# Q and K weights loaded as two column halves with x between them, two pads on VectorE, new orders on every engine

## The chip, the cores and the metric

The kernel runs on one core of a Trainium2 chip. The core has five engines that run beside each other, each with its own queue of instructions: TensorE (matmuls; PE in the profile, PEld for its weight loads), VectorE (DVE), ScalarE (ACT), GpSimd (POOL) and SyncE (SP), which here only issues DMA transfers. The metric is the device time of one execution in microseconds. Before the change it is 194.48 us, the median of three runs (193.82 to 194.73).

## The reference

The input x has 2048 rows of 448 columns. The block is a linear-attention layer followed by a gated MLP, each behind a layer norm and with a residual:

```python
phi = lambda t: where(t > 0, t + 1, exp(t)) + 1e-6
q, k, v = split(layernorm(x) @ wqkv)          # 16 heads of 28 columns
kv  = phi(k)^T v          # per head
z   = sum over rows of phi(k)
o   = (phi(q) kv) / (phi(q) z + 1e-6)
h   = x + o @ wo
n   = layernorm(h)
out = h + (gelu(n @ w_gate) * (n @ w_up)) @ w_down     # 1792 inner columns
```

Inputs and the output are bf16.

## The kernel before, in words

The 2048 rows are 16 tiles of 128 rows, numbered 0 to 15. The work has three stretches.

*Attention, first pass (0 to about 34 us).* Each tile of x is loaded (`dx0`, `dx1`, `dx2` for tiles 2 and 3, then `dx4`, `dx8`, `dx12` for four tiles each). Its layer norm is `bnst1_t` and `bnag1_t` on VectorE (lines 409 and 410) and `ln1_t`, `rstd1_t` on ScalarE (416 and 418). The normed rows are made by VectorE for tiles 0 to 3 (`normD_t`, line 431) and transposed by TensorE (`tr0_t` and `tr1_t`, line 439), from where ScalarE and VectorE copy one half each (`evxA_t`, `evxD_t`, lines 444 and 446). For tiles 4 to 15 POOL makes them (`negm1_t`, `normP_t`, lines 413 and 449), and a DMA transpose on SP turns them round (`xT_t`, line 451). The K projection of a tile is `k_t` (four matmuls, line 465), followed by `ek_t` on ScalarE (476) and `ck_t`, `pk_t` on VectorE (477 and 478). The sum over rows that the key-value product needs is gathered by `pt4_t`, or by `pt1_t` and `pt3_t` from tile 10 on (line 484). The Q projection is `q_t`, followed by `eq_t` and `rq_t` on ScalarE (492 and 493), and later by `cq` and `aq` on VectorE.

*The middle (about 34 to 53 us).* `z1`, `z0`, the copies `evp`, `kv` (line 523), `kvm` (527), `w2_0` to `w2_3` (543) with copies `evw` (547 and 549). For the rows: products with z (`t1`, on POOL from row tile 1 on, lines 565 and 581), their sums (`dr`, 568 and 582), the reciprocal (`de`, `rd`) and the scaled rows (`pn`, 572 and 586). For the first pair of tiles TensorE transposes these (`tro`, 595), and `out1` (613) multiplies by w2; later pairs are transposed by DMA (`oT_p`, 601) and multiplied in two halves, `outA_p` and `outB_p` (623 and 624), which need copies of w2 made by two DMAs, `dws0` and `dws1`. `hr_t` (629) adds x; a second norm follows (`bnst2`, `bnag2`, `vpe2`, `pow2`, `negm2`, and `nhD` or `nhP`), `wrap_t` on VectorE (660) doubles the row, and a DMA transpose `hT_t` (661) turns it round. For tiles 0 and 1 TensorE does it (`trh`, 650), with the copies `evhA_0` and `evhD_1`.

*The MLP (53 us to the end).* `gu2_v` and `gu4_v` (lines 722 and 724) are 56 tasks of gate and up matmuls, two half-height matmuls side by side; `ge` on ScalarE (742) and `hm` on VectorE (744) take their results from PSUM, two buffers in turn. `gu2` 0 to 6 serve tiles 0 and 1, 7 to 13 tiles 2 and 3, `gu4` 14 to 27 tiles 4 to 7, 28 to 41 tiles 8 to 11, 42 to 55 tiles 12 to 15. `downA_p` and `downB_p` (692) are the down projection of a pair of tiles, `fo` (698 and 678) adds h, and `do_t` stores the tile. The last two tiles have their own matmuls (674), tile 15 in two column halves.

What sets the order: every operation is a task, numbered in the order in which the code adds it, and `ORDERS` (lines 15 to 49) lists the tasks of each engine in the order in which they are emitted. Nothing is reordered at run time: an instruction that waits holds back everything after it on its engine. The waits come from `_Graph` (lines 69 to 226), which derives them from the buffers that a task reads and writes; a task with several slots (`mw`) waits within itself, so that `q_t` asks for the second half of the transposed tile only at its third matmul and for the last rows of the weights only at its fourth. `HOLD` picks which of several waits is issued first.

Lines that the change touches: the padding memsets and the loads (361 to 373), the helpers `dma_w3` and `dma_w1` (351 to 355: the weights' first 384 rows in three blocks, and the 64 rows left), `proj_reads`, `k_tile`, `q_tile` (468 to 493), `fkv` (519 to 526), `ORDERS` and `HOLD`. Since dwqk_t writes the buffer that the memset wqkpad has written (`b_wqk[1]`), the load waits for the memset.

Of the kernel before, what the change touches and what calls it, by code (L numbers as in the profile page):

```python
# [813 lines left out]
```

## Time and profile before

| what | value |
|---|---|
| three runs | 193.82, 194.48, 194.73 us; median 194.48 |
| profiled execution | 194.29 us, of which the span of its instructions is 192.5 |
| TensorE busy | 185.7 us, 96% of the span; granted clock 1.00 throughout |
| VectorE, ScalarE, POOL busy | 131.5, 77.0, 52.4 us |
| first matmul after the warm-up | 5.39 us |
| x of tiles 2 and 3 landed | 6.91 us |
| k_2 starts | 10.40 us |
| k_7 starts | 21.31 us |
| last K task (pt1_15) over, q_5 starts | 33.61 us |
| first gate/up task (gu2_0) starts | 53.39 us |
| last matmul ends | 190.09 us |

How to read it: the rows of time in the profile are instructions grouped by line; a start and a duration in microseconds from the start of the span, then engine, line, operation, and what was written from what. Where a task is named, it was found by counting the instructions of its engine along `ORDERS`. A matmul's shown duration includes its way through the array, so consecutive matmuls overlap; the step from one start to the next is what TensorE spends: 0.76 us for a `k_t`, `q_t` or `pt4_t`, 1.51 for a `gu` task, 2.65 for a `down` half. The 40 matmuls of the warm-up, 1.04 to 5.49 us, count as busy.

### The profile page before, as it was taken

To read this page: it belongs to the slowest core of one execution; us is meant where nothing else is said; L and a number is where in the kernel's file an instruction comes from. 1 tells how busy PE (TensorE), PEld (TensorE's weight loads), DVE (VectorE), ACT (ScalarE), POOL (GpSimd) and SP (SyncE) were. 2 spreads that over 40 slices of the span, in tenths; PEclk is the share of its full clock that TensorE was granted. 3 is DMA by queue.
4 is the path that set the end of the run, shared out by engine and by line. 5 is a ranking of instruction groups with operands and counts; after the bars stand their busy time and mean duration, and the time that the engine had idled before them with its cause. 6 is when DMAs were issued, how large, how long until landed. Compare 5 with 4: busy or idle time off the path is not lost.

```text
span 192.5 us, 4453 instructions
## 1 busy us (share of the span) xinstructions
PE 185.7 (96%) x1813; PEld 115.3 (60%) x1813; DVE 131.5 (68%) x326; ACT 77.0 (40%) x220; POOL 52.4 (27%) x93
## 2 busy tenths in 40 slices
PE   7999899988999999999999999999999999999995
PEld 7545355544578878975788745556445455555643
DVE  2899997899999986898958774528544624415232
ACT  3798643777992411333214431421442414211200
POOL 8067650740048193340008600001800000000000
PEclk9999999999999999999999999999999999999999
DMA  5974558994388500772200391000095100000045
GB/s 181 382 207 70 100 109 176 220 219 92 84 193 243 95 3 14 86 143 51 48 0 3 60 161 21 2 3 24 0 136 60 51 0 0 3 0 0 3 140 170
DMA packets 34596, 17.11 MB, mean 89 GB/s; under 512 B 26832, under 2 KB 33168, under 8 KB 34576
## 3 DMA queue, kind: packets, MB, share of 16 engines
q1 hardware_dynamic: 34432, 16.72, 39.9%
q8 instruction: 14, 0.23, 0.6%
q10 hardware_dynamic: 144, 0.11, 0.2%
q14 instruction: 6, 0.05, 0.1%
HBM read 8.26 MB, written 1.84 MB: 52 GB/s over the span
## 4 chain that ended last, share of the span: by engine, by line
PE 83%; DVE 8%; DMA 4%; POOL 1%; issue 1%; ACT 1%; SPq 0%; POOLq 0%
PE ps L724 32%; PE ps L692 18%; PE ps L722 13%; PE ps L465 8%; PE ps L484 4%; PE ps L674 3%; PE ps L623 3%; DMA x_sb<-in_A_x_dram 2%; DMA xnT<-xnn 2%; PE ps L624 2%; DVE st L409 1%; DVE den L568 1%; DVE pqn L572 1%; DVE eq L578 1%; PE ps L613 1%
## 5 line engine op out<-in xcount | busy, mean ns | idle before, releaser
L724 PE MATMUL ps<-hnT,wgu_sb 64*128 64x512 bf16 (+1 forms) x490 | 88.7, 333 | 0.0
L722 PE MATMUL ps<-hnT,wgu_sb 64*128 64x512 bf16 (+1 forms) x490 | 88.6, 333 | 0.0
L742 ACT ACTIVATE gl<-ps 128x256 bf16<-128x256 f32 x112 | 36.8, 382 | 83.2 <-PE ps L722 83.2
L744 DVE TENSOR_TENSOR hh<-ps,gl 128x256 bf16<-128x256 f32 x112 | 43.1, 416 | 37.0 <-ACT gl L742 36.8
L724 PEld LDWEIGHTS ps<-hnT,wgu_sb 64*128 64x128 bf16 x490 | 45.1, 94 | 26.2 <-DVE hh L744 2.7
L722 PEld LDWEIGHTS ps<-hnT,wgu_sb 64*128 64x128 bf16 x490 | 45.5, 94 | 5.0 <-DVE hnT L656 0.2
L692 PE MATMUL ps<-wd_sb,hh 64*128 64x448 bf16 x392 | 41.6, 349 | 0.3 <-DVE hh L744 0.3
L692 PEld LDWEIGHTS ps<-wd_sb,hh 64*128 64x128 bf16 x392 | 24.3, 94 | 13.7 <-DVE hh L744 1.3
L465 PE MATMUL ps<-wqk_sb,xnT 128*128 128x448 bf16 x128 | 27.5, 353 | 0.9 <-DMA xnT<-xnn 0.9
L409 DVE BATCH_NORM_STATS2 st<-x_sb 128x6 f32<-128x448 bf16 x32 | 19.1, 614 | 3.8 <-DMA x_sb<-in_A_x_dram 3.7
L465 PEld LDWEIGHTS ps<-wqk_sb,xnT 128*128 128x128 bf16 x128 | 12.1, 98 | 12.3 <-DMA xnT<-xnn 1.3
L581 POOL TENSOR_TENSOR t<-pq,zbc 128x448 f32<-128x448 bf16 x12 | 12.6, 1068 | 16.2 <-DVE pq L579 16.2
L698 DVE TENSOR_TENSOR x_sb<-ps,x_sb 128x448 bf16<-128x448 f32 x14 | 8.4, 618 | 8.9 <-PE ps L692 8.9
L484 PE MATMUL ps<-pk,xnn 128*128 128x448 bf16 x64 | 14.2, 352 | 0.0
L623 PE MATMUL ps<-w,pqnT 64*128 64x448 bf16 x49 | 11.5, 349 | 0.1
L476 ACT ACTIVATE e<-ps 128x448 bf16<-128x448 f32 x16 | 8.7, 541 | 6.7 <-PE ps L465 6.3
L413 POOL TENSOR_SCALAR nm<-mv 128x1 f32<-128x1 f32 (+1 forms) x19 | 4.1, 228 | 25.9 <-DVE mv L410 25.5
L449 POOL TENSOR_SCALAR xnn<-x_sb,nm,rs 128x448 bf16<-128x448 bf16 x12 | 9.6, 797 | 4.6 <-ACT rs L418 4.3
L658 POOL TENSOR_SCALAR hn<-x_sb,nm,rs 128x448 bf16<-128x448 bf16 x14 | 10.4, 751 | 0.5
L624 PE MATMUL ps<-pt_sb,pqnT 64*128 64x448 bf16 x42 | 10.2, 350 | 0.0
L629 DVE TENSOR_TENSOR x_sb<-ps,x_sb 128x448 bf16<-128x448 f32 x16 | 9.7, 614 | 0.7 <-PE ps L624 0.7
L421 POOL TENSOR_SCALAR ln<-mv 128x2 f32<-128x2 f32 x7 | 1.5, 223 | 31.3 <-DVE mv L410 31.1
(83 smaller groups left out, 167.0 us busy)
## 6 DMA issues: line engine op xcount, KB each, us to landing
out_dram<-x_sb SPq DMA_DIRECT2D x15, 112.0 KB, 1.8
wd_sb<-in_B_w_down_dram SPq DMA_DIRECT2D x1, 1568.0 KB, 7.5
x_sb<-in_A_x_dram SPq DMA_DIRECT2D x3, 448.0 KB, 5.6
wgu_sb<-in_B_w_gate_dram SPq DMA_DIRECT2D x1, 896.0 KB, 12.3
wgu_sb<-in_B_w_up_dram SPq DMA_DIRECT2D x1, 896.0 KB, 15.7
wqk_sb<-in_A_wqkv_dram SPq DMA_DIRECT2D x1, 672.0 KB, 4.7
wgu_sb<-in_B_w_gate_dram SPq DMA_DIRECT2D x1, 672.0 KB, 6.2
wgu_sb<-in_B_w_up_dram SPq DMA_DIRECT2D x1, 672.0 KB, 8.7
```

The lines of the kernel that those rows point to most:

```text
L409: op("dve", lambda e: e.bn_stats(st[:, t, :], src_ap), [b_src], [b_st[t]], "bnst%s_%d" % (tag, t))
L465: ins = e.matmul(ps[:, bk, 0:D], xnT[:, t, k, :], wqk_sb[:, k, c0:c0 + D], start=(k == 0), stop=(k == 3))
L484: ins = e.matmul(ps[:, BK_PT[c], 0:D], xnn[:, t % XN_R, c * 128:(c + 1) * 128], pk[:, ip, :], start=(t == 0), stop=(t == T - 1))
L581: op("pool", lambda e, n=n: e.tensor_tensor(t1[:, n, :], pq[:, a + n, :], zbc[:, :], ALU.mult), [b_pq[a + n]] + b_z, [b_t1[n]], "t1p_%d" % ...
L623: e.matmul(ps[:, BK_OUT[0], 0:D], pqnT[ra, i2, sg // 2, :], w2[ra, sg // 2, :], start=(sg == 0), stop=(sg == 5))
L624: ins = e.matmul(ps[:, BK_OUT[1], 0:D], pqnT[rb, i2, 3 + (sg + 1) // 2, :], (w2 if sg == 6 else w2s)[rb, sg // 2, :], start=(sg == 0), sto ...
L658: op("pool", lambda e, t=t, sh=sh: e.tensor_scalar(hn[:, sh, 0:D], x_sb[:, t, :], nm2[:, t:t + 1], rs2[:, t:t + 1], ALU.add, ALU.mult), [b ...
L692: ins = e.matmul(ps[:, BK_O[n], 0:D], hh[rows, j, sl[n]], wd_sb[rows, j, :], start=(half == 0 and j == 0), stop=(half == 1 and j == NJ - 1))
L722: first = e.matmul(psG[:, jj * N:(jj + 1) * N], wgu_sb[A_, k, j * 128:(j + 1) * 128], hnT[A_, ka_, c0:c0 + N], start=(k == 0), stop=(k == ...
L724: ins = e.matmul(psU[:, jj * N:(jj + 1) * N], wgu_sb[B_, k, j * 128:(j + 1) * 128], hnT[B_, kb_, c0:c0 + N], start=(k == 0), stop=(k == NK ...
L742: G.add("act", lambda e, gi=gi, cs_=cs_, psG=psG: e.activation(gl[:, gi, cs_], psG[:, cs_], AF.Gelu_apprx_tanh), r=[b_ps[BK_G[i]]], w=[b_g ...
L744: op("dve", lambda e, dst=dst, srcU=srcU, srcL=srcL: e.tensor_tensor(dst, srcU, srcL, ALU.mult), [b_ps[BK_U[i]], b_glh], [b_ar[j_][t % HR] ...
```

## The change

The code, without the lists of orders:

```diff
-        b_wqk, b_wv = bufs("wqk", 2), bufs("wv", 2)
+        b_wq, b_wk, b_wv = bufs("wq", 2), bufs("wk", 2), bufs("wv", 2)
+        b_wpad = bufs("wpad", 2)
...
         def dma_w3(q, dst, c0, c1, b, name):
-            return dma(q, dst[:, 0:3, :], A_wqkv[0:384, c0:c1].rearrange("(k p) n -> p k n", p=128), [b[0]], name)
+            return dma(q, dst[:, 0:3, c0 % (2 * D):c0 % (2 * D) + c1 - c0], A_wqkv[0:384, c0:c1].rearrange("(k p) n -> p k n", p=128), [b[0]], name)
...
-        for dst, b, nm_ in ((wqk_sb, b_wqk, "wqkpad"), (wv_sb, b_wv, "wvpad")):
-            op("pool", lambda e, dst=dst: e.memset(dst[:, 3, :], 0.0), [], [b[1]], nm_)
+        for dst, b, nm_ in ((wqk_sb, b_wpad[0], "wqkpad"), (wv_sb, b_wpad[1], "wvpad")):
+            op("dve", lambda e, dst=dst: e.memset(dst[B_, 3, :], 0.0), [], [b], nm_)
         dma_x("sp", 0, 1)
-        tx1 = dma_x("act", 1, 2)
-        dma_w3("sp", wqk_sb, 0, 2 * D, b_wqk, "dwqk")
-        dma_w1("sp", wqk_sb, 0, 2 * D, b_wqk, "dwqk_t")
+        dma_x("act", 1, 2)
+        dma_w3("sp", wqk_sb, 0, D, b_wq, "dwq")
+        dma_w1("act", wqk_sb, 0, D, b_wq, "dwq_t")
         dma_x("sp", 2, 4)
+        dma_w3("sp", wqk_sb, D, 2 * D, b_wk, "dwk")
+        tx1 = dma_w1("act", wqk_sb, D, 2 * D, b_wk, "dwk_t")
         dma_x("sp", 4, 8)
...
-        def proj_reads(t):
-            return [(b_xnT[t][0], 0), (b_xnT[t][1], 2), (b_wqk[0], 0), (b_wqk[1], 3)]
+        def proj_reads(t, b):
+            return [(b_xnT[t][0], 0), (b_xnT[t][1], 2), (b[0], 0), (b[1], 3), (b_wpad[0], 3)]
...
-            G.add("pe", lambda e, W: proj(e, W, t, bk, D), r=proj_reads(t), w=[b_ps[bk]], name="k_%d" % t, mw=True)
+            G.add("pe", lambda e, W: proj(e, W, t, bk, D), r=proj_reads(t, b_wk), w=[b_ps[bk]], name="k_%d" % t, mw=True)
...
-        G.add("pe", fkv, r=b_wv + b_pt, w=[b_ps[BK_KV]], name="kv")
+        G.add("pe", fkv, r=b_wv + [b_wpad[1]] + b_pt, w=[b_ps[BK_KV]], name="kv")
```

The Q weights (`dwq`) and the K weights (`dwk`) are separate loads into the same tile, with x of tiles 2 and 3 between them; their last 64 rows (`dwq_t`, `dwk_t`) are issued by ScalarE, ahead of its table load (`tbl1`, line 392). The pads are set by VectorE, on the 64 partitions that the load does not write, and have buffers of their own.

The orders are all new. The stretches that matter, by name:

```
loads on SP
 before  dx0 dwqk dwqk_t dx2 dx4 dx8 dx12 dwv dwv_t dwo
 after   dx0 dwq dx2 dwk dx4 dx8 dx12 dwv dwv_t dwo
start of ScalarE
 before  dx1 tbl1 ln1_0 rstd1_0 ln1_1 rstd1_1 evxA_0 evxA_1 rq_0 eq_0 ln1_2
 after   dx1 dwq_t dwk_t tbl1 ln1_0 rstd1_0 ln1_1 evxA_0 rstd1_1 ln1_2 rstd1_2 eq_0 evxA_1
VectorE, first tiles
 before  bnst1_0 bnag1_0 bnst1_1 bnag1_1 normD_0 normD_1 evxD_0 evxD_1 bnst1_2 bnst1_3 ...
         ck_2 bnst1_9 bnst1_7 bnag1_9 bnag1_7 bnst1_8 pk_2 bnst1_10 ck_3
 after   wqkpad bnst1_0 bnag1_0 bnst1_1 normD_0 bnag1_1 bnst1_2 evxD_0 bnag1_2 normD_1 bnst1_3
         normD_2 bnag1_3 evxD_1 bnst1_4 bnst1_5 bnag1_4 normD_3 ...
         bnst1_9 bnst1_10 bnag1_9 ck_2 bnag1_10 pk_2 bnst1_8 bnst1_7 ck_3 bnag1_7 ... pk_9 wvpad ck_10
TensorE, first tiles
 before  warm tr1_0 tr0_0 tr1_1 tr0_1 q_0 k_0 k_1 q_1 tr0_2 tr1_2 tr1_3 tr0_3 k_2 q_2 pt4_0
 after   warm tr0_0 tr1_0 q_0 tr1_1 tr0_1 k_0 tr0_2 tr1_2 k_1 q_1 tr0_3 tr1_3 k_2 q_2 pt4_0
TensorE, end of the K tiles to the first gate/up task
 before  k_15 k_14 pt1_11 pt1_12 pt3_10 pt1_13 q_4 pt1_14 pt1_15 q_5 pt3_11 pt3_12 pt3_13 pt3_14
         pt3_15 q_7 q_9 kv q_6 q_11 w2_1 w2_0 w2_2 w2_3 tro_0 q_10 tro_1 out1_0 q_8 out1_1 q_13 q_15
         q_12 q_14 trh_0 trh_1 outA_1 outB_1 gu2_0
 after   k_14 pt3_10 k_15 pt1_11 pt1_12 pt1_13 pt3_11 pt3_12 pt1_14 pt1_15 pt3_13 pt3_14 pt3_15 q_4
         q_5 kv q_9 q_7 w2_1 w2_0 q_8 w2_2 w2_3 tro_0 q_6 tro_1 out1_0 q_11 out1_1 q_10 q_13 q_15
         q_14 outA_1 trh_0 trh_1 q_12 outB_1 gu2_0
VectorE, the same stretch
 before  evpD_3 z0 t1d_0 dr_0 rd_0 dr_1 cqP_2 evpD_2 dr_2 dr_3 aqP_2 pn_0 kvm rd_3 kvd rd_1 pn_3
         evwD_1 rd_2 pn_1 evwD_3 pn_2 drP_2 hr_0 ... cqP_4 nhD_0 ... evhD_1
 after   evpD_3 z0 aq_1 t1d_0 evpD_2 dr_0 dr_1 rd_1 kvm dr_2 cqP_2 kvd rd_0 dr_3 pn_0 evwD_1 pn_1
         rd_3 rd_2 evwD_3 pn_2 pn_3 aqP_2 hr_0 bnst2_0 hr_1 bnag2_0 bnst2_1 bnag2_1 drP_2 nhD_0 ... evhD_1
TensorE, around the change of tiles in the MLP
 before  outB_4 gu2_13 downA_1 gu4_14 gu4_15 outA_5 gu4_16 outB_5 gu4_17 downB_1 outA_6 gu4_18 ...
         gu4_27 downA_2 gu4_28 outA_7 gu4_29 outB_7 gu4_30
 after   gu2_13 outB_4 gu4_14 gu4_15 gu4_16 gu4_17 gu4_18 outA_5 gu4_19 outB_5 gu4_20 gu4_21 downA_1
         outA_6 gu4_23 outB_6 gu4_22 downB_1 gu4_25 outA_7 gu4_24 outB_7 gu4_27 gu4_26 gu4_29 gu4_28 downA_2
VectorE, places of the wraps in the MLP
 before  wrap_3 hr_5 wrap_2 bnst2_4 hm1_4 hm0_4 ... hr_12 wrap_8 wrap_11 hm0_23 hm1_23 wrap_9 wrap_10
 after   hm1_4 wrap_2 hm0_4 bnst2_4 cqP_4 hm0_5 wrap_3 ... hm1_20 wrap_8 wrap_9 hr_12 bnst2_12 hm1_23
         hm0_23 bnag2_12 hr_13 fo448_3 hm0_22 wrap_10 wrap_11 hm1_22
VectorE, the last gate/up results
 before  hm1_55 hm1_54 hm0_54 hm0_55
 after   hm0_55 hm1_54 hm0_54 hm1_55
end of TensorE
 before  downA_6 down224_15 downB_6 down448_14 down224_15
 after   downA_6 down448_14 downB_6 down224_15 down224_15
end of SP
 before  ... do_13 do_2 do_10 do_14 do_15
 after   ... do_8 do_10 do_14 do_0 do_5 do_11 do_6 do_9 do_7 do_2 do_13 do_12 do_15 do_15
```

On POOL the two memsets go out; `t1p_5` and `t1p_4` change places, `mones`, `mask_a` and `mask_b` move behind the norms of the K tiles, and `vpe2_6` moves ahead of `nhP_5`. On SP the copies `dws0` and `dws1` go ahead of `oT_1`.

## The prediction

> **What bounds the kernel now.** I read the page first, then TensorE's waits, then the chain of waits over the first 24 us, the DMA issues, and the order of time on each engine.
>
> ```profile
> span 192.5 us, 4453 instructions
> ...
> PE 185.7 (96%) x1813; PEld 115.3 (60%) x1813; DVE 131.5 (68%) x326; ACT 77.0 (40%) x220; POOL 52.4 (27%) x93
> ...
> PE 83%; DVE 8%; DMA 4%; POOL 1%; issue 1%; ACT 1%; SPq 0%; POOLq 0%
> ```
>
> TensorE is busy for all but 6.8 us, and 1.04 of that is before its first matmul and 2.4 after its last. So a reorder can win only the holes in between and the small slips that the modelled ends hide. The waits name the holes:
>
> ```profile
> PE ps L465 <- DMA xnT<-xnn: 0.9, 1, 0.9
> PE ps L595 <- DVE w L549: 0.9, 1, 0.9
> PE ps L523 <- ACT eq L492: 0.6, 1, 0.6
> PE ps L439 <- DVE xnn L431: 0.6, 2, 0.3
> ```
>
> The chain over the first 24 us shows what each hole hangs on. The reader is to see that the second issue of x waits behind a padding memset, and that VectorE then waits for its landing:
>
> ```profile
> 1.09 0.78 POOL wqk_sb L362
> 1.88 0.58 POOL xnn L382
> 2.45 0.03 SPq L344
> ...
> 2.53 4.38 DMA x_sb<-in_A_x_dram
> ...
> 6.93 1.15 DVE st L409 x2
> ...
> 16.96 0.72 POOL xnn L449
> ...
> 17.69 3.57 DMA xnT<-xnn
> ...
> 21.31 0.93 PE ps L465 x4
> ```
>
> The last line is k_7. By stages (the table of windows: start and end, length, busy us of PE, PEld, DVE, ACT, POOL), VectorE is the tight engine from 33.6 to 53.4 us, and TensorE alone after 87 us:
>
> ```profile
> 33.60:53.40 19.80, 18.20 (x129) 9.64 (x129) 18.93 (x39) 16.22 (x39) 6.55 (x7) 1.00 0.73 151
> ...
> 87.30:190.10 102.80, 102.79 (x982) 59.62 (x980) 54.52 (x137) 28.09 (x86) 12.48 (x22) 1.00 0.22 41
> ```
>
> **The change, part by part.** Times are those of the profiled execution (194.29 us, span 192.5), which is 0.19 below the median of the three runs, 194.48; the sum is a difference and is laid on the median.
>
> *Loads.* Before, dx2 (x of tiles 2 and 3) is issued at 2.53, behind dwqk (672 KB) and dwqk_t (112 KB); dwqk_t waited for the padding memset that ended at 1.88. Now 336 KB of Q weights stand ahead of it, its end is on ScalarE's queue, and the pad has a buffer of its own. So dx2 is issued at about 1.24 + 0.42 (an SP issue) = 1.7.
>
> ```profile
> wqk_sb<-in_A_wqkv_dram SPq DMA_DIRECT2D x1, 672.0 KB, 4.7
> ...
> x_sb<-in_A_x_dram SPq DMA_DIRECT2D x1, 224.0 KB, 4.4
> ...
> x_sb<-in_A_x_dram SPq DMA_DIRECT2D x1, 112.0 KB, 2.7
> ```
>
> Its landing is bounded by 1.7 + 2.7 = 4.4 (the row of the first tile, nothing ahead) and 1.7 + 4.4 = 6.1 (as now). The bytes ahead fall by 392 KB, at the 382 GB/s of the page's second slice 1.0 us, and the issue is 0.8 earlier. The two overlap: I take 5.5 instead of 6.91. Half rows cost nothing by the packet records: 896 B took 40 to 41 ns, 1792 B 74 to 84. dwk then lands at about 6.6, and k_0 is due at 7.2. x of tiles 4 to 7 keeps its place in the bytes (8.03).
>
> *ScalarE's queue.* Two more issues (0.39 to 0.58 each, with gaps 0.9 to 1.4) push the table load from 1.22 to about 2.4. It takes 1.28; ScalarE idled 1.86 before ln1_0 at 4.36. Cost nothing, 0.5 left; beyond it each tenth delays normD_0 by as much.
>
> *Padding.* POOL loses 0.85 and 0.47, inside its first 5 us, followed by 4.4 idle: nothing. VectorE gets wqkpad in the 3.48 us in which it waits for x: nothing. wvpad falls after pk_9, where VectorE is dense. No memset of VectorE's is in the trace: between 0.25 (cq, 128x448) and 0.47 (POOL's); I take 0.3, absorbed below.
>
> *First tiles.* VectorE now has bnst1_2 ahead of evxD_0 and normD_1, so both wait for dx2, and with them q_0's third matmul and tr_1. From dx2 at 5.5: bnst1_2 to 6.05, evxD_0 to 6.3 (q_0 starts 6.2, before 6.44), normD_1 6.4, bnst1_3, normD_2 7.65, evxD_1 7.95, bnst1_4, bnst1_5, normD_3 9.6, ck_0, evxD_2 10.1. TensorE: q_0, tr_1, k_0 7.2, tr_2 8.0, k_1 8.2, q_1, tr_3 9.7, k_2 at 10.05 instead of 10.40: −0.35 (between +0.2, dx2 at 6.1, and −0.6).
>
> *The hole before k_7.* k_9 would end at 19.9. VectorE now takes bnst 10 and 8 and pk_2 ahead of bnst1_7 (0.55 each): bnag1_7 at 15.6 instead of 13.9. Then ln, rstd, normP_7 to 17.4, and transpose 7 at 17.4 against 17.69, since SP no longer meets it late behind the others. It lands 2.5 (median) to 3.6 us later: 19.9 to 21.0, against 21.26. I take 20.0, nearest the median. k_8 is thus over at 23.0, with pt4_6 already in; before, that point was 24.34: −1.3 in all from here back (−0.2 to −1.5).
>
> *To the end of the K tiles* (pt1_15): 9.65 us of TensorE work to 32.65 against 33.61, although pt3_11 and pt3_12 (1.14) have come in and q_4 (0.76) has gone out. VectorE needs its last pk by 32.2: six ck and pk pairs, cq_1, aq_3, wvpad from 26.0 make 31.9. −0.95.
>
> *From there to gu2_0.* Before 19.78: 17.5 of TensorE work and 2.3 of stalls, behind VectorE. Work is now 17.1 (the exchange above). On VectorE aq_1 comes in (0.37) and cqP_4 goes out (0.36), and two slow instructions should shrink:
>
> ```profile
> 36.52 2.04 POOL L565 TENSOR_TENSOR t<-pq,zbc 128x448 f32<-128x448 bf16 x2
> ...
> 37.19 1.62 DVE L578 TENSOR_SCALAR eq<-eq 128x896 bf16<-128x896 bf16 x1
> ...
> 49.58 0.36 DVE L578 TENSOR_SCALAR eq<-eq 128x896 bf16<-128x896 bf16 x1
> ```
>
> cqP_2 took 1.62 beside POOL's products and its like 0.36 alone; it now stands after kvm and dr_2, when POOL's t1p_3 is over. pn_3 (1.36 beside t1p_4, others 0.55) now precedes those products. That is −1.26 and −0.8 at most. Against it, aqP_2 stands late and drP_2 waits for t1p_4, and dr_1 and rd_1 wait for POOL and ScalarE ahead of kvm. I take 18.3 (17.1 if no stall is left, 19.8 if the same): −1.45. The Trainium skill, "SBUF — State Buffer", section "Who interferes with whom", says that VectorE's two-port modes and POOL lock each other out for a whole instruction; by that rule the 1.26 goes, and were 1.62 the form's own time the sum would be 1.26 worse. The trace agrees, with 0.36 for the same form.
>
> *From gu2_0 to the last matmul.* The same work. Before it took 136.7 us with slips I read from starts: downA_1 took 3.29 for 2.65, downA_6 2.95. downA_1 now comes after gu4_21 with its inputs long there: −0.64; hm0_54 is third, not fourth: −0.2. But wrap_2 (behind nhP_2) now stands ahead of hm0_4, and wrap_8 and wrap_9 ahead of hr_12 and hm1_23: VectorE waits there for POOL, about 3 us at wrap_8. By my working hm_22 is 0.25 late for gu4_24, and transpose 13 0.3 late for gu4_43; two or three such slips more I put at 0.5. Net +0.2 (−1 to +2).
>
> *End.* SP holds eleven stores behind do_14, which is ready 4.65 before the last matmul ends, 0.48 apart; the last issues at 0.63 after the last matmul instead of 0.45: +0.2 (0 to 0.5).
>
> Sum: −0.95 − 1.45 + 0.2 + 0.2 = −2.0; **192.5 us**.
>
> **Rivals.**
>
> *The early gain is eaten* (0.20). Transpose 7 lands late again (3.6 us, and normP_7 held 0.3 more behind ScalarE's eq_2, rq_2): k_7 at 21.3, pt1_15 at 33.9, and the middle keeps its 2.3 of stalls: gu2_0 near 53.3. With +0.4 behind it, 194.7. For it: two more bnst ahead of tile 7. Against: tile 7's transpose waited 1.4 us for its turn before.
>
> *The split does not bring x forward* (0.07). dx2 lands at 6.9 after all, if the engines share out packets of all queues alike. Then bnst1_2 holds evxD_0 and q_0's third matmul till 7.75, 1.0 us worse at k_2 than before; some is lost in the wait at k_7: 193.8. Against it: 0.8 us of earlier issue is plain. The Trainium skill, "DMA: Bandwidth & Descriptors", section "Queues, rings and completion order", says that each transfer engine takes turns between the queues packet by packet. By that rule dwk_t would go beside dx2, an estimate of 0.2 us on its landing; no run here shows it.
>
> *Slower: transposes of the normed h land after their turn* (0.15). downA_1 and downB_1 no longer stand ahead of gu4_14 and gu4_28. By my working the last landings lead their gate/up tasks by 0.3 (gu2_7), 1 (gu4_14), 0.9 (gu4_29) and −0.3 (gu4_43). Landings took 3.0 to 5.0 us here. At 1.5 later than worked, each border costs its shortfall: 1.2 + 0.5 + 0.6 + 1.8, less the 0.3 already counted, +3.8: 196.3. It decides from about 1.3 later. Against it: only the three last transposes took over 4.4.
>
> *Nearly all stalls go* (0.08): 17.4 from pt1_15 to gu2_0 and −0.5 behind: 190.9.
>
> **Numbers.** The forecast has 0.50, its own range 191.5 to 193.5. A measurement here tells about 0.5% from no change, 193.5 to 195.45. Faster: 0.50 + 0.08 + half of the split case, 0.61. Same: 0.20 and the rest of it, 0.23. Slower 0.16. The range 190.9 to 195.6 leaves out most of the slower case and a little below.
>
> **What would show it.** x of tiles 2 and 3 landing at 5.5 and k_2 near 10.0; k_7 near 20 with a wait under 0.3; cqP_2 under 0.5 us; gu2_0 near 51; few waits of TensorE from VectorE's hh or a transpose after that. The prediction is wrong if gu2_0 is not before 52.5, or if TensorE from gu2_0 to its end takes over 138 us: then hm rows behind a wrap, or hnT transposes, stand in TensorE's waits.

## The result, and the profile after

The changed kernel takes 193.62 us (median of 20 runs, 192.50 to 194.67) against 194.30 us for the kernel before on the same chip (20 runs, 193.16 to 194.73). The ratio is 0.9963, with a 95% interval of 0.9946 to 0.9981: 0.7 us faster, where 2.0 was forecast. The time lies inside the range given, but the gain is about a third of the forecast.

The profiled execution took 193.84 us. From its page, the span, the busy time of the engines and the shares of the chain of work that ended last:

```profile
span 191.9 us, 4456 instructions
...
PE 185.7 (97%) x1813; PEld 107.3 (56%) x1813; DVE 128.4 (67%) x328; ACT 75.2 (39%) x220; POOL 50.7 (26%) x91
...
PE 79%; DVE 11%; DMA 4%; ACT 3%; POOL 0%; SPq 0%; issue 0%
```

TensorE's busy time is the same 185.7 us. All that could be won was idle time, and the span is shorter by 0.6 us (192.49 to 191.86). TensorE's waits (engine, line, what was waited for, total us, times, longest) show what idle time is left:

```profile
PE ps L407 <- POOL ones_bf L379: 1.0, 1, 1.0
PE ps L627 <- DVE hn L647: 0.8, 1, 0.8
PE ps L726 <- DVE x_sb L702: 0.7, 1, 0.7
PE ps L469 <- DMA xnT<-xnn: 0.4, 1, 0.4
PE ps L469 <- DVE xnT L450: 0.4, 1, 0.4
PE ps L469 <- ACT xnT L448: 0.3, 1, 0.3
```

The waits for VectorE's `w` (0.9, at tro_0), for ScalarE's `eq` (0.6, at kv) and for VectorE's `xnn` (0.6) are gone, and that for transpose 7 is halved. In their place are new ones: at q_0's start and inside it (the last two rows), ahead of outA_1 (the second) and ahead of gu4_43 (the third). Behind the second and third stands a DMA transpose, as the landing times below show, though the profile names the waiter that came last by its records.

The chain of waits over the first 24 us (start, length, what; line numbers of the changed kernel are two higher than before's at the loads and four higher from the warm-up on):

```profile
1.24 0.42 SPq L346
1.71 4.70 DMA x_sb<-in_A_x_dram
6.43 0.63 DVE st L413
...
8.71 1.06 DVE st L413 x2
9.86 0.28 DVE xnn L435
...
16.83 0.94 POOL xnn L453 x2
17.77 3.41 DMA xnT<-xnn
21.23 0.93 PE ps L469 x4
```

The padding memset has left the chain and the issue of dx2 is 0.82 us earlier, as forecast. But dx2 landed at 6.41, not 5.5, and the transpose of tile 7 still takes 3.41 us, so k_7 starts where it did (21.23 against 21.31).

By stages (windows: start and end, length, busy us of PE, PEld, DVE, ACT, POOL, then granted clock, DMA share, GB/s), the two that answer to those shown of before:

```profile
33.93:52.14 18.21, 17.40 (x126) 9.52 (x125) 16.71 (x39) 16.15 (x40) 8.59 (x10) 1.00 0.88 170
...
87.30:189.33 102.03, 101.31 (x970) 51.67 (x966) 51.88 (x131) 26.12 (x82) 12.28 (x22) 1.00 0.19 37
```

The first stage is 1.57 us shorter: TensorE's stalls there fell from 1.6 to 0.8 us, its busy time from 18.20 to 17.40, and VectorE's from 18.93 to 16.71. In the second, TensorE was busy without a break before (102.79 of 102.80), and now stands 0.7 us.

| where (us) | before | forecast | after |
|---|---|---|---|
| dx2 landed | 6.91 | 5.5 | 6.41 |
| dx4 landed | 8.03 | 8.03 | 8.48 |
| k_2 starts | 10.40 | 10.05 | 10.63 |
| k_7 starts | 21.31 | 20.0 | 21.23 |
| pt1_15 over | 33.61 | 32.65 | 33.93 |
| pt1_15 to gu2_0 | 19.78 | 18.3 | 18.21 |
| gu2_0 starts | 53.39 | 51.0 | 52.14 |
| gu2_0 to the last matmul's end | 136.70 | 136.9 | 137.19 |
| behind it, to the span's end | 2.40 | 2.6 | 2.53 |

So the K stage lost 0.3 us where 0.95 was to be won; the middle won what was forecast; the MLP lost 0.5 where 0.2 was forecast. VectorE's timeline over the first tiles (start, duration; in brackets the idle time before and what ended it):

```profile
6.43 0.63 DVE L413 BATCH_NORM_STATS2 st<-x_sb 128x6 f32<-128x448 bf16 x1 [1.19 <-DMA x_sb<-in_A_x_dram]
6.97 0.28 DVE L450 COPY xnT<-ps 128x256 bf16<-128x256 bf16 x1
...
7.25 0.36 DVE L435 TENSOR_SCALAR xnn<-x_sb,mv,rs 128x448 bf16<-128x448 bf16 x1
...
8.63 1.14 DVE L413 BATCH_NORM_STATS2 st<-x_sb 128x6 f32<-128x448 bf16 x2
...
9.78 0.36 DVE L435 TENSOR_SCALAR xnn<-x_sb,mv,rs 128x448 bf16<-128x448 bf16 x1
```

The rows are bnst1_2, evxD_0, normD_1, then bnst1_4 with bnst1_5, then normD_3. VectorE idles 1.19 us for dx2 while evxD_0 and normD_1, which need no byte of it, stand behind. So q_0's second half starts only at 7.30, and from there to k_2 at 10.63 TensorE works without a hole: in this execution k_2 is late because dx2 is. And bnst1_4 starts 0.15 after dx4 has landed (8.48): had everything before it been earlier, it would have waited for that load. In the MLP, SP's queue around the transposes of the last tiles:

```profile
137.13 1.22 SPq L665 DMA_TRANSPOSE hnT<-hn  x1
138.40 0.58 SPq L703 DMA_DIRECT2D out_dram<-x_sb  x1
139.02 1.23 SPq L665 DMA_TRANSPOSE hnT<-hn  x1
140.29 0.58 SPq L703 DMA_DIRECT2D out_dram<-x_sb  x1
140.92 3.62 SPq L665 DMA_TRANSPOSE hnT<-hn  x2
```

These are hT_14, do_3, hT_15, do_4, and hT_12 with hT_13. The last one, issued at 143.24, landed at 146.22, and gu4_43 starts at 146.27. At the pace of the matmuls of downB_3 it was due at 145.18, so it is 1.09 us late (the wait in the list, 0.7, counts from a modelled end). Two stores, which nothing in this stretch waits for, stand between the transposes.

### The profile page after: what moved, and what is told of

The parts are those of the page before. It is cut to its first block, busy times and chain, and to the rows that moved or that the text cites. A ratio compares the mean times of both kernels' runs of the same rounds, so it can differ in the third digit from the quotient of the medians.

```text
span 191.9 us, 4456 instructions
## 1 busy us (share of the span) xinstructions
PE 185.7 (97%) x1813; PEld 107.3 (56%) x1813; DVE 128.4 (67%) x328; ACT 75.2 (39%) x220; POOL 50.7 (26%) x91
## 4 chain that ended last, share of the span: by engine, by line
PE 79%; DVE 11%; DMA 4%; ACT 3%; POOL 0%; SPq 0%; issue 0%
PE ps L728 38%; PE ps L696 19%; PE ps L726 7%; PE ps L469 4%; PE ps L488 3%; PE ps L678 3%; PE ps L627 3%; DMA x_sb<-in_A_x_dram 2%; DVE st L413 2%; PE ps L628 2%; DMA xnT<-xnn 2%; DVE pqn L576 1%; DVE den L572 1%; ACT e L480 1%; DVE x_sb L633 1%; DVE w L553 1%
## 5 line engine op out<-in xcount | busy, mean ns | idle before, releaser
L748 DVE TENSOR_TENSOR hh<-ps,gl 128x256 bf16<-128x256 f32 x112 | 42.4, 416 | 38.6 <-ACT gl L746 38.4
L696 PEld LDWEIGHTS ps<-wd_sb,hh 64*128 64x128 bf16 x392 | 21.8, 94 | 15.8 <-issue 0.4
L469 PE MATMUL ps<-wqk_sb,xnT 128*128 128x448 bf16 x128 | 28.2, 355 | 1.0 <-DMA xnT<-xnn 0.4
L482 DVE SCALAR_TENSOR_TENSOR pk<-ps,e 128x448 bf16<-128x448 f32 x16 | 9.9, 619 | 0.2
L453 POOL TENSOR_SCALAR xnn<-x_sb,nm,rs 128x448 bf16<-128x448 bf16 x12 | 8.9, 743 | 3.5 <-ACT rs L422 2.9
```

Of the source, the lines that this page charges most:

```text
L469: ins = e.matmul(ps[:, bk, 0:D], xnT[:, t, k, :], wqk_sb[:, k, c0:c0 + D], start=(k == 0), stop=(k == 3))
L696: ins = e.matmul(ps[:, BK_O[n], 0:D], hh[rows, j, sl[n]], wd_sb[rows, j, :], start=(half == 0 and j == 0), stop=(half == 1 and j == NJ - 1))
L748: op("dve", lambda e, dst=dst, srcU=srcU, srcL=srcL: e.tensor_tensor(dst, srcU, srcL, ALU.mult), [b_ps[BK_U[i]], b_glh], [b_ar[j_][t % HR] ...
```

## The experiments

All times below are medians of several runs, and the ratios are to the kernel before on the same chip; versions that ran on different chips are compared by these ratios; starts and landings come from the one profiled execution of each kernel. None leaves out or changes any of what is computed. In the diffs the orders are written by the tasks' names.

### The first tiles

**VectorE's wait for dx2 put behind work that doesn't need it.** In the changed kernel:

```diff
 VectorE
-... bnag1_1 bnst1_2 evxD_0 bnag1_2 normD_1 bnst1_3 ...
+... bnag1_1 evxD_0 normD_1 bnst1_2 bnag1_2 bnst1_3 ...
 ScalarE
-... rstd1_2 eq_0 evxA_1 ...
+... rstd1_2 evxA_1 eq_0 ...
```

> The changed kernel with bnst1_2 and bnag1_2 moved behind evxD_0 and normD_1 on VectorE, and evxA_1 ahead of eq_0 on ScalarE, so that the copy for q_0 and the norm of tile 1 no longer stand behind the wait for x of tiles 2 and 3. Theory 1 (the early gain was lost to that wait): q_0's four matmuls go through from 6.2 without the 0.74 us pause, k_2 starts at about 10.2 instead of 10.63, and what is gained there reaches gu2_0 (52.14 in the changed kernel): 51.6 to 51.8, 0.3 to 0.5 us less in all. Theory 2 (the stretch up to k_8 is set by the transposes of tiles 6, 9 and 7, which are slow around the 16 KB instruction fetch at 15.26 us): k_2 comes at 10.2 all the same, but k_7 stays at 21.0 to 21.3 and gu2_0 at 52.0 to 52.3, so no change in time.

Measured 193.67 us, ratio 0.9978 (0.9961 to 0.9995). evxD_0 ran at 5.96 and normD_1 at 6.25, and q_0 was over by about 6.95 without its pause. But k_2 started at 10.69, no earlier than the changed kernel's 10.63. In this execution dx2 landed at 6.75 and dx4 at 8.78, and VectorE's timeline shows both waits, one right behind the other:

```profile
6.77 0.63 DVE L413 BATCH_NORM_STATS2 st<-x_sb 128x6 f32<-128x448 bf16 x1
...
8.80 1.15 DVE L413 BATCH_NORM_STATS2 st<-x_sb 128x6 f32<-128x448 bf16 x2
...
9.95 0.36 DVE L435 TENSOR_SCALAR xnn<-x_sb,mv,rs 128x448 bf16<-128x448 bf16 x1
```

The rows are bnst1_2, then bnst1_4 with bnst1_5, then normD_3. bnst1_4 starts as dx4 lands. normD_3, 1.15 us behind it, is not what k_2 waits for here: the transposes of tile 3, which need it, start at 10.42, right behind q_1. k_2 starts 0.42 after evxA_2, the copy of its own tile on ScalarE (10.27), which stands behind ln1_4, and that needs bnst1_4 and so dx4. TensorE had also stood for dwk ahead of k_0 and for normD_2, on dx2, ahead of tile 2's transposes. So the first theory, that the wait for dx2 alone makes k_2 late, does not hold as it stood: that wait is real, but others lie right behind it. How much is due to dx2, which came 0.34 later than in after, this run can't tell.

**The last rows of the K weights on SP, behind dwk,** instead of on ScalarE's queue beside dx2:

```diff
-        dma_w1("act", wqk_sb, 0, D, b_wq, "dwq_t")
+        tx1 = dma_w1("act", wqk_sb, 0, D, b_wq, "dwq_t")
...
-        tx1 = dma_w1("act", wqk_sb, D, 2 * D, b_wk, "dwk_t")
+        dma_w1("sp", wqk_sb, D, 2 * D, b_wk, "dwk_t")
```

> The changed kernel with the last 64 rows of the K weights (dwk_t) issued on SP behind dwk instead of on ScalarE. In the changed kernel x of tiles 2 and 3 landed at 6.41 us, 4.7 after its issue, although half the bytes stood ahead of it. Theory A (dwk_t on the other queue takes turns with it on the engines that they share): it lands at 5.5 to 5.9 now, VectorE's wait of 1.19 us ahead of bnst1_2 falls to 0.3 to 0.7, and k_2 starts at 10.0 to 10.3. Theory B (the landing is late because the loads ahead are as slow as before, whatever queue): it stays within 6.2 to 6.5. dwk_t lands at 7.5 to 7.9, still before k_0 needs it or 0.2 later. Time: 0 to 0.4 us less by A, the same by B.

Measured 193.21 us, 0.9961 (0.9934 to 0.9989). dx2 landed at 6.01, dx4 at 8.59, and k_2 started at 10.50. That settles nothing: with the same loads and dwk_t on ScalarE's queue, dx2 landed at 5.89 to 6.57 in the other profiles of this study, besides the 6.41 of after and the 6.75 above.

**The loads and pads of the change, in before's orders:**

```diff
 SP       (kernel before)
-dx0 dwqk dwqk_t dx2 dx4 ...
+dx0 dwq dx2 dwk dx4 ...
 ScalarE
-dx1 tbl1 ...
+dx1 dwq_t dwk_t tbl1 ...
 POOL
-wqkpad wvpad ...
 VectorE
+wqkpad ... pk_9 wvpad ...
```

> The kernel before in its own orders with only the loads and pads of the change: dx0 dwq dx2 dwk on SP, dwq_t and dwk_t on ScalarE, wqkpad first and wvpad after pk_9 on VectorE. If the loads alone are worth something: x of tiles 2 and 3 lands at 6.4 instead of 6.91, tiles 2 and 3 are normed 0.4 earlier, and k_2 comes at 10.0; k_0 (7.19 before) now waits for dwk at 7.3 and is 0.2 late. If the transposes around the instruction fetch set the end of this stretch, k_7 stays at 21.0 to 21.5, gu2_0 at 53.2 to 53.6, and the time is that of the kernel before within 0.3 us.

Measured 194.12 us, 0.9997 (0.998 to 1.0014): the loads by themselves are worth nothing. dx2 landed at 6.57, dx4 at 8.53, k_2 started at 10.66 and gu2_0 at 53.54 (53.39 before). What before's order waits for at k_2 is no longer dx2.

### x behind the K weights, and x ahead of all weights

The question left was whether x between the halves matters at all, and whether an early x would help. **dx2 behind dwk** in the changed kernel (the edge that keeps a queue's loads in the order of the code is dropped, so that the list alone orders them; likewise in the two kernels below that load dx2 first):

```diff
-            ... kind="dma", after=list(after) + last[q])
+            ... kind="dma", after=list(after))
 SP
-dx0 dwq dx2 dwk dx4 ...
+dx0 dwq dwk dx2 dx4 ...
```

> The changed kernel with x of tiles 2 and 3 issued behind the K weights on SP again (dx0 dwq dwk dx2), all else as changed: undoes the one thing that the split is made for. If bringing x forward is worth what I forecast (dx2 1.4 us earlier): dx2 lands at 7.2 to 7.6 instead of 6.0 to 6.7, VectorE holds evxD_0 and normD_1 behind it, k_2 starts at 11.2 to 11.7 instead of 10.6, and the kernel is 0.4 to 1.0 us slower than the changed one. If the stretch up to k_8 is set by the transposes of tiles 6 to 7 and by x of tiles 4 to 7, k_2 is later but k_7 stays within 21.0 to 21.7, and the time is the same within 0.3 us.

Measured 195.05 us, 1.0064 (1.0038 to 1.009): 1.0% slower than the changed kernel. dx2 landed at 7.34, and VectorE shows the wait:

```profile
7.37 0.63 DVE L413 BATCH_NORM_STATS2 st<-x_sb 128x6 f32<-128x448 bf16 x1 [1.99 <-DMA x_sb<-in_A_x_dram]
```

k_2 started at 11.57 and gu2_0 at 52.94, 0.9 and 0.8 later than in after, and the last matmul ended 1.2 later. In the new orders a late dx2 is paid for, since bnst1_2 stands ahead of evxD_0 and normD_1.

**dx2 ahead of dwq**, together with the stores' move of the next part (with which it is to be compared, 0.9924):

```diff
 SP
-dx0 dwq dx2 dwk dx4 ...
+dx0 dx2 dwq dwk dx4 ...
...
-hT_14 do_3 hT_15 do_4 hT_12 hT_13
+hT_14 hT_15 hT_12 hT_13 do_3 do_4
```

> The kernel with the two stores moved, and x of tiles 2 and 3 issued on SP ahead of the Q weights too (dx0 dx2 dwq dwk). Theory (k_2 follows the landing of x of tiles 2 and 3 by 4.2 us, as it did at 6.41 and 10.63, 6.01 and 10.24): it lands at 4.6 to 5.2, VectorE's wait ahead of bnst1_2 is gone, the Q weights land at 5.4 to 6.1, in time for q_0 at 6.2 or 0.3 late, k_2 starts at 9.6 to 9.9, k_7 at 20.2 to 20.6, and the kernel is 0.3 to 0.7 us faster than with the stores alone (192.67, 0.9924 of the kernel before). Rival (x of tiles 4 to 7, which lands at 8.0 to 8.8 whatever stands ahead, sets normD_3 and with it k_2): normD_3 stays at 9.4 to 9.9, k_2 at 10.2 to 10.6, and nothing is gained.

Measured 192.77 us, 0.995 (0.9932 to 0.9967), so not faster than without. dx2 landed at 4.24, 2.2 us earlier than in after, yet k_2 started at 10.47. VectorE, and behind it ScalarE's ln1_4 and evxA_2:

```profile
7.32 0.29 DVE L450 COPY xnT<-ps 128x256 bf16<-128x256 bf16 x1
8.58 1.15 DVE L413 BATCH_NORM_STATS2 st<-x_sb 128x6 f32<-128x448 bf16 x2 [0.97 <-DMA x_sb<-in_A_x_dram]
...
9.73 0.36 DVE L435 TENSOR_SCALAR xnn<-x_sb,mv,rs 128x448 bf16<-128x448 bf16 x1
```

```profile
9.85 0.30 ACT L420 ACTIVATE ln<-mv,eps_t 128x1 f32<-128x1 f32 x1 [0.68 <-DVE mv L414]
10.05 0.36 ACT L448 ACTIVATE xnT<-ps 128x256 bf16<-128x256 bf16 x1
```

Now VectorE stands 0.97 us for dx4, which landed at 8.55. This shows the limit at k_2: dx4's landing plus bnst1_4 and bnst1_5, and behind them two things at once, normD_3 for the transposes of tile 3 (10.15) and, on ScalarE, ln1_4 with the copy evxA_2, 0.42 us ahead of k_2. From dx2 to the start of bnst1_4 the changed kernel took 2.2 us (6.41 to 8.63), so an earlier dx2 is worth nothing once it lands 2.2 us ahead of dx4, which is at about 6.3.

### The stores between the transposes

```diff
 SP
-hT_14 do_3 hT_15 do_4 hT_12 hT_13
+hT_14 hT_15 hT_12 hT_13 do_3 do_4
```

> The changed kernel with the stores do_3 and do_4 on SP moved behind the last transpose hT_13. In the changed kernel gu4_43 stood still for 1.09 us until 146.27, and the transpose of tile 13 landed at 146.22; the two stores took 1.2 us of SP's time between the transposes. If they are the cause: hT_13 lands 1.0 to 1.3 us earlier, gu4_43 starts at 145.2 to 145.4, right behind downB_3, and the kernel is 0.8 to 1.1 us faster than the changed one. If the 16 KB instruction fetch at 141 us sets the landing: hT_13 gains under 0.5 us and so does the kernel. If the wait was for VectorE's fo448_6 and fo448_7, as the list of waits names it, nothing changes.

Measured 192.67 us, 0.9924 (0.9901 to 0.9947). SP's timeline for the same stretch:

```profile
136.78 6.18 SPq L665 DMA_TRANSPOSE hnT<-hn  x4
143.00 1.08 SPq L703 DMA_DIRECT2D out_dram<-x_sb  x2
```

hT_13 landed at 144.65 instead of 146.22, gu4_43 started at 144.85 right behind downB_3, and gu2_0 to the last matmul took 136.13 instead of 137.19. The two stores cost the changed kernel about 1.06 us. In this execution k_2 also came 0.39 earlier (dx2 landed at 6.01, dx4 at 8.08), which the edit doesn't touch.

### The hole before k_7

TensorE's instructions are fetched in blocks of 16 KB: the page counts 14 packets on queue q8, kind "instruction", and the packet records give the time of each. The first is fetched at 14.64 in before and at 15.26 in after, while the transposes of x are in flight. A theory was that this fetch delays them, and through SP's queue k_7. The fetch follows the count of TensorE's instructions, so fewer warm-up matmuls move it. **Twenty warm-up matmuls of 512 columns instead of 40 of 128:**

```diff
-    WARM = 40
+    WARM = 20
...
-                ins = e.matmul(ps[:, 3, 0:128], ones_bf[:], ones_bf[:], start=True, stop=True)
+                ins = e.matmul(ps[:, 3, 0:512], ones_bf[:], ones_bf[:].unsqueeze(1).to_broadcast([128, 4, 128]), start=True, stop=True)
```

> The changed kernel with the warm-up made of 20 matmuls of 512 columns instead of 40 of 128 (the same 4.3 us or so, 40 instructions of TensorE fewer, counting their weight loads). If the 16 KB instruction fetch at 15.3 us belongs to TensorE's stream, it comes some five tasks of eight instructions later, at 18.5 to 19.5 us. Theory (transposes in flight beside that fetch land late): transpose 6 lands 2.5 us after its issue instead of 4.3, SP spends 1.3 us on transpose 9 instead of 2.4, transpose 7 is issued by 17.7 at the latest (POOL has normP_7 done at 17.68) and is now the one that may be hit: k_7 at 20.3 if it is not, 21.3 if it is. Rival (these transposes are slow for another reason, such as the loads of weights still in flight): the fetch moves and transposes 6 and 9 are as slow as before, k_7 at 21.2. Time: 0 to 0.8 us less than the changed kernel.

Measured 194.89 us, 1.0038 (1.0018 to 1.0058). The fetch moved to 17.81, but the warm-up no longer fitted: it ran until 7.65 instead of 5.49, and k_2 started at 11.95. The wait before k_7 stayed: k_2 to k_7 took 10.49 against 10.60. **The same, with the norm of tile 7 as early as in before:**

```diff
 VectorE
-... bnst1_9 bnst1_10 bnag1_9 ck_2 bnag1_10 pk_2 bnst1_8 bnst1_7 ck_3 bnag1_7 ...
+... bnst1_9 bnst1_7 bnst1_10 bnag1_9 bnag1_7 ck_2 bnag1_10 pk_2 bnst1_8 ck_3 ...
 ScalarE
-... rstd1_9 ... ln1_7 rstd1_7 ...
+... rstd1_9 ln1_7 rstd1_7 ...
 POOL
-... negm1_9 ... normP_9 ... negm1_7 ... normP_7 ...
+... negm1_9 negm1_7 ... normP_9 normP_7 ...
```

> The kernel with the later fetch, and the norm of tile 7 taken as early as in the kernel before (bnst1_7 right behind bnst1_9 on VectorE, its steps on ScalarE and POOL likewise). Theory (fetch and the late norm of tile 7 together hold k_7): normP_7 is done by 16.4, transpose 7 is issued at 16.7 to 17.0 and lands by 19.5, ahead of the fetch; k_7 follows k_9 without a hole, at 20.5 to 20.8, and the kernel is 0.4 to 1.0 us faster than the changed one. Rival (VectorE's total work holds the K stretch, so that a hole closed at k_7 opens behind it): k_7 at 20.6, but pt1_15 stays at 33.4 to 33.9 and the time is the same.

Measured 194.71 us, 1.004 (1.0019 to 1.006). The transpose of tile 7 was issued 6.12 us after k_2's start instead of 7.14, but it landed only at 22.27, 4.53 us later: the fetch, at 18.77, now lay beside it. **Ten matmuls of 512 columns:**

```diff
-    WARM = 40
+    WARM = 10
...
 (the matmul of 512 columns, as above)
```

> The changed kernel with a warm-up of 10 matmuls of 512 columns. In the run with 20 of them each took 0.427 us until about 5.5 us and 0.216 from then on, so 10 take 4.3 us, as the 40 short ones do now (0.107 each), with 60 instructions of TensorE fewer. Theory (the 16 KB fetch is TensorE's, and transposes beside it are slow): the fetch comes 5 to 6 us later, at 20.5 to 21.5; transpose 6 lands 2.5 us after its issue, SP spends 1.3 us on transpose 9, transpose 7 goes out at 17.7 and lands at 20.2, k_7 starts at 20.2 to 20.5 instead of 21.23, ten to 10.0 us behind k_2 instead of 10.6, and the kernel is 0.5 to 0.9 us faster than the changed one. Rival (VectorE's stream holds k_7 to pt1_15): k_7 is earlier, pt1_15 stays at 33.5 to 33.9 and so does the time.

Measured 195.59 us, 1.0092 (1.0064 to 1.012). The warm-up ended at 5.49 as before and k_2 started at 10.25, so this is the clean form of the test. The fetch came at 19.71, again beside transpose 7. From issue to landing, in us, with the time of the 16 KB fetch:

| kernel | fetch at | transpose 6 | transpose 9 | transpose 7 |
|---|---|---|---|---|
| before | 14.64 | 3.45 | 2.48 | 3.57 |
| after | 15.26 | 4.29 | 3.68 | 3.41 |
| x behind dwk | 16.16 | 4.28 | 3.72 | 3.17 |
| 20 long matmuls | 17.81 | 2.52 | 3.75 | 3.60 |
| and tile 7 early | 18.77 | 2.55 | 2.44 | 4.53 |
| 10 long matmuls | 19.71 | 2.52 | 2.52 | 4.88 |

The transposes in flight beside the fetch are the slow ones, and move with it: transposes 6 and 9 took 3.45 to 4.3 us beside it and 2.4 to 2.6 when it lay elsewhere, and transpose 7 took 4.5 to 4.9 beside it. So the fetch does delay transposes. But it does not explain k_7 in the changed kernel: there it lies before transpose 7 is issued, and transpose 7 took 3.2 to 3.6 us in all four kernels of the table whose fetch does not lie in the middle of its flight.

The packet records hold another fetch there. The page counts a second queue of kind "instruction", q14, with 8 KB a packet, and one such packet starts 1.2 to 2.0 us after the issue of transpose 7 in each of these four kernels (19.58 in before, 19.02 in after). The 14 traces of this study have 168 transposes of x. The 57 with no fetch of either kind in their first 2.45 us landed 2.4 to 3.1 us after their issue, and every slower one had a fetch there. With an 8 KB fetch that started 1.1 to 2.1 us after the issue, and no 16 KB one, 22 of 23 took 3.15 to 3.65 us; with one that started earlier or later, 55 of 56 took 2.4 to 2.95. So transpose 7's 3.41 us in after fits this second fetch. No run moves it, so it is not shown to be the cause.

The last kernel also showed what a longer hole costs. TensorE waited 2.11 us for transpose 7, and the granted clock (third number from the end of a row of windows) then fell to a half:

```profile
22.00:23.00 1.00, 0.63 (x3) 0.32 (x4) 0.00 (x0) 0.00 (x0) 0.00 (x0) 0.80 0.68 134
23.00:24.00 1.00, 1.00 (x4) 0.37 (x3) 0.00 (x0) 0.10 (x1) 0.00 (x0) 0.50 0.44 84
...
25.00:26.00 1.00, 1.00 (x4) 0.41 (x3) 1.00 (x2) 0.00 (x0) 1.00 (x3) 0.50 0.60 123
26.00:27.00 1.00, 1.00 (x7) 0.54 (x6) 0.00 (x1) 0.00 (x0) 0.33 (x2) 0.99 0.00 0
```

At that rate a block of four matmuls of 448 columns takes twice its time, and gu2_0 started at 55.13, 3.0 later than in after. This profiled execution took 197.04 us, 1.45 above the median of its six, so the fall may not come in every run.

### One instruction of the middle, alone

The kernel before, with VectorE's cqP_2 moved behind dr_3 and nothing else:

```diff
 VectorE
-... rd_0 dr_1 cqP_2 evpD_2 dr_2 dr_3 aqP_2 ...
+... rd_0 dr_1 evpD_2 dr_2 dr_3 cqP_2 aqP_2 ...
```

> The kernel before with one instruction moved: cqP_2 on VectorE behind dr_3 instead of ahead of evpD_2, when POOL's products t1p_2 and t1p_3 are over (38.56 us). Theory (the middle gained because cqP_2 no longer runs beside them): it takes 0.36 to 0.45 us instead of 1.62, evpD_2 and dr_2 come 1.3 to 1.5 us earlier, kv loses its wait of 0.56, tro_0 starts at 43.2 to 43.7 instead of 44.43, and gu2_0 at 52.3 to 52.8 instead of 53.39: the kernel is 0.5 to 1.0 us faster than before. Rival (1.62 us is what this form costs at this place, or ScalarE's round trips hold the chain): it stays over 1 us, or gu2_0 within 0.3 us of 53.39.

Measured 193.48 us, 0.9971 (0.9955 to 0.9987). VectorE's timeline (evpD_2, dr_2 with dr_3, cqP_2):

```profile
37.58 0.62 DVE L517 CAST pt_sb<-ps 128x448 bf16<-128x448 f32 x1
38.12 1.26 DVE L568 TENSOR_REDUCE den<-t 128x16 f32<-128x448 f32 x2
39.30 0.38 DVE L578 TENSOR_SCALAR eq<-eq 128x896 bf16<-128x896 bf16 x1
```

cqP_2 took 0.38 us instead of 1.62, evpD_2 ran 1.15 earlier, kv started at 38.89 instead of 39.44, tro_0 at 43.84 instead of 44.43, gu2_0 at 52.81 instead of 53.39. This one move brings about as much as the whole change (0.9971 against 0.9963, within each other's intervals), whose larger gain in the middle is partly lost elsewhere. It accounts for 0.58 us of the 1.57 by which the middle got shorter; the rest was not taken apart by a run, and 0.38 of it is TensorE work that moved from this stage into the K stage. pn_3, which the move leaves beside POOL's next products, still took 1.36 us here.

### Can more be had?

**q_12 ahead of outA_1**, with the stores moved: TensorE waits 0.98 us at outA_1 for the transpose oT_1 (issued 43.83, landed 49.01 in after), and q_12 needs none of it.

```diff
 TensorE
-... q_13 q_15 q_14 outA_1 trh_0 trh_1 q_12 outB_1 gu2_0
+... q_13 q_15 q_14 q_12 outA_1 trh_0 trh_1 outB_1 gu2_0
 SP
 (as in the part on the stores)
```

> The kernel with the two stores moved, and q_12 on TensorE ahead of outA_1 instead of behind the transposes trh. In the changed kernel TensorE stood 0.98 us ahead of outA_1, until 49.05, while oT_1, issued at 43.83, landed at 49.01, behind the gate and up weights that landed at 47.36. Theory: q_12 fills the hole, outA_1 starts at 49.0, and gu2_0 is then bound by evhD_1 (51.53): 51.6 to 51.8 at the same head, 0.3 to 0.5 us less than with the stores alone. Rival (evhD_1, behind pnP_2 on VectorE, comes later too, since trh does): gu2_0 within 0.15 of where it was.

Measured 192.39 us, 0.9923 (0.99 to 0.9946), against 0.9924 for the stores alone. gu2_0 came 0.37 earlier than there, of which k_2 gave 0.06; the last matmul ended 0.40 earlier. The trace shows some 0.3 us and the times can't tell it from nothing. It is the fastest version that was run: 1.5 us less than the kernel before on the same chip (193.88).

**All together**: dx2 first, the stores moved, q_12 moved, and normD_3 ahead of bnst1_4 (with ScalarE's rstd1_3 ahead of rq_0), so that k_2 would wait for neither load:

```diff
 VectorE
-... evxD_1 bnst1_4 bnst1_5 bnag1_4 normD_3 ...
+... evxD_1 normD_3 bnst1_4 bnst1_5 bnag1_4 ...
 SP
-dx0 dwq dx2 dwk dx4 ...
+dx0 dx2 dwq dwk dx4 ...
```

> The kernel with the two stores moved, q_12 in the hole, x of tiles 2 and 3 issued first, and normD_3 on VectorE ahead of bnst1_4 and bnst1_5 (rstd1_3 on ScalarE ahead of rq_0), so that tile 3 no longer stands behind the wait for x of tiles 4 to 7. With x issued first alone, x of tiles 2 and 3 landed at 4.24 and bnst1_4 still waited until 8.58 for x of tiles 4 to 7, normD_3 came at 9.73 and k_2 at 10.47. Theory (that wait, with normD_3 queued behind it, set k_2): normD_3 comes at 7.4 to 8.0, k_2 at 9.8 to 10.1 right behind q_1, k_7 at 20.4 to 20.8, gu2_0 at 51.0 to 51.2, and the time is 0.3 to 0.6 us below that with stores and q_12 moved (0.9923 of the kernel before): 0.989 to 0.991. Rival (the transposes from tile 4 on hold everything from k_4 on, whenever k_2 comes): k_2 at 10.0, but k_7 stays at 20.8 to 21.1 and the time at 0.992.

Measured 193.58 us (191.88 to 194.37), 0.9975 (0.9951 to 0.9999), 1.2 slower than the version above. Two rows of TensorE's waits:

```profile
PE ps L469 <- DMA wqk_sb<-in_A_wqkv_dram: 1.0, 2, 0.7
PE ps L627 <- DMA pqnT<-pqn: 1.0, 1, 1.0
```

normD_3 ran at 9.01, 0.77 earlier than in after. But q_0 and k_0 now wait for the weights (dwq landed at 6.44, dwk at 8.21), and k_2 started at 11.23. Of that, 0.25 is a wait for evxA_2: with normD_3 moved ahead of it, bnst1_4 ran only at 9.34, and ln1_4 with evxA_2 behind it on ScalarE at 10.61 and 10.81. A version with evxA_2 ahead of ln1_4 was not run. The second row is outA_2's: its transpose oT_2 landed 4.85 us after its issue, where it took 2.9 to 3.0 in before, in after and in the version above. Why it was slow in this execution was not settled.

## Why the prediction was right or wrong

**Right.** The middle: 18.21 us against 18.3 forecast, with cqP_2 at 0.41 and pn_3 at 0.61 us. The rows of POOL's products and of cqP_2 in the changed kernel:

```profile
37.39 2.03 POOL L569 TENSOR_TENSOR t<-pq,zbc 128x448 f32<-128x448 bf16 x2
...
39.26 0.41 DVE L582 TENSOR_SCALAR eq<-eq 128x896 bf16<-128x896 bf16 x1
```

cqP_2 now starts at 39.26, as POOL's products end (at 39.42); in before it lay beside them from 37.19 and ended at 38.81, 0.25 after them. The one-move kernel shows for cqP_2 that its place beside them made it slow. By the rule of the Trainium skill, "SBUF — State Buffer", section "Who interferes with whom", the 1.26 us were to go; the 0.38 us for the moved instruction agree. For pn_3 the shorter time was measured only in the whole change. That 18.3 was met within 0.1 is partly luck, since it was a choice between 17.1 and 19.8 and not a sum: the 1.24 us that cqP_2 lost in the one-move kernel were worth 0.58 at gu2_0. Also as forecast: the ScalarE queue (the first rows of norms ran at 4.19, earlier than the 4.36 of before), both pads (0.43 us in VectorE's wait, and 0.24 after pk_9), downA_1 (its slip of 0.64 is gone) and the end (2.53 against 2.6). From k_8's end to pt1_15 the 9.65 us of TensorE's work came out at 9.66.

**Wrong: "First tiles", k_2 at 10.05.** It started at 10.63, 0.58 later than forecast and just past the upper bound of the step. The step that failed is the landing of dx2: through evxD_0 and q_0's pause it set k_2 in this execution. Two landings were taken as one value each where they have a spread. dx2 landed at 6.41, not 5.5, past its own upper bound of 6.1 too; with the same loads it landed between 5.89 and 6.75. And dx4 "keeps 8.03" was assumed; it landed between 8.00 and 8.78. The working had bnst1_4 and bnst1_5 ahead of normD_3, but took dx4 to land as early as before. It also left out that evxA_2 stands behind ln1_4, and so behind dx4, on ScalarE. The run with dx2 at 4.24 shows that even a perfect dx2 would have given k_2 at about 10.5 with dx4 at 8.55.

**Wrong: "The hole before k_7", k_7 at 20.0.** It started at 21.23. Of these 1.2 us, 0.37 is the later issue (17.77 for 17.4, which follows from the later norms), and the rest the landing: the median of all transposes, 2.5, was taken, although tile 7's own row of before said 3.57. It took 3.41, with an 8 KB instruction fetch in its flight in before and after alike; that this is why is not shown. The forecast expected the issue to come earlier because SP would no longer meet it late. In before it did wait for SP, from normP_7's end at 16.31 to 17.69 (the POOL row ahead of transpose 7 in the chain shown of before is normP_8). In after POOL and SP were due together: normP_7 ended at 17.68, and transpose 9, beside the 16 KB fetch, held SP until 17.73. So the wait for SP went, but the later norms took its place. The rival "the early gain is eaten" had this part right (k_7 at 21.3, pt1_15 at 33.9; measured 21.23 and 33.93), and was wrong only in the stalls of the middle, which did go.

**Wrong in size: "transpose 13 0.3 late for gu4_43".** 1.09 us. The mechanism was right. What was missing are the two stores between the transposes, 0.62 us of SP's time each, and hT_12, which held SP for 2.28 us instead of some 1.25, beside a 16 KB fetch at 141.05. The stores alone were shown by moving them. (The rival on late landings reads that only the three last transposes took over 4.4 us in before; of the three that did, one was issued at 78.23, in mid-MLP, and the last of all took 4.35.) downA_1's gain of 0.64 made up part of it. The other terms did not come: TensorE has no other hole of over 0.1 us from gu2_0 to its end, so the 0.25 at gu4_24 and the 0.5 for further slips were not there, and the 0.2 to be won at downA_6 was misread, since it takes 2.95 us to the next task's start before and after alike. So the whole of the MLP came to +0.5 instead of +0.2.

Together: 0.58 at k_2, 0.65 from there to k_7, 0.3 in the MLP, less 0.1 in the middle: 1.4 of the 2.0 us forecast. Moving x between the weight halves is not idle in the new orders, since putting it back behind costs 1.0%; but before's orders, with the same loads, gain nothing from it. What pays is the middle. Whether dwk_t on ScalarE's queue delays dx2, and why the same loads land up to 0.9 us apart, stays open.

## What to carry to other kernels

On an engine that works in order, an instruction that waits for a load holds all behind it: put it behind whatever doesn't need that load, and look for the next load that will be waited for before counting the gain. Take the time of a transfer from its own row, not from the median of its kind, look at what else is fetched during its flight, and give it the spread that it has between executions. In a queue of transposes that feeds TensorE, stores go last; and before reordering everything, look for the one instruction whose duration is a multiple of its like, since moving it alone may give most of the gain.
